# A gated mix of a diagonal state-space layer and a SiLU FFN on one core: the order of TensorE's stages, the place of its transpositions, the cut of the last readout and the choice of PSUM banks are changed

## The chip, the cores and the metric

The kernel runs on one core of one Trainium2 chip. The core has five engines that run side by side, each through its own queue in order: TensorE (PE in the profile; its weight loads are shown apart as PEld), VectorE (DVE), ScalarE (ACT), GpSimd (POOL) and SyncE (SP). SP and POOL here mostly issue DMAs. TensorE writes only to PSUM, which has eight banks of 128 partitions; VectorE or ScalarE must copy a bank out before it can be written again. The metric is the device time of one execution in microseconds (us), median of several runs; lower is better.

## The reference

The input x has 2048 tokens of 448 features. Two branches read it, and a gate mixes them token by token.

```python
g = sigmoid((x * gate_w).sum(-1))                 # one number a token
# branch a: a diagonal complex recurrence of 448 states
Lam = Lambda_re + 1j*Lambda_im;  dt = exp(log_dt);  Lam_bar = exp(dt*Lam)
B_bar = ((Lam_bar - 1)/Lam)[:, None] * (B_re + 1j*B_im)
Bu = x @ B_bar.T
for t in range(2048):  h = Lam_bar*h + Bu[t];  hs.append(h)
a = 2*real(hs @ (C_re + 1j*C_im).T) + x*Dskip
# branch b: a feed-forward layer, 448 -> 1792 -> 448
b = silu(x @ w1) @ w2
out = g*a + (1 - g)*b
```

## The kernel before

**Chunks and slots.** The tokens are taken in four chunks of 512 (tc = 0 to 3), and each chunk in four blocks of 128 (tb = 0 to 15). The 448 complex states are 896 real rows, held in seven slots of 128.

**TensorE's kinds of work.** The text uses these names:

- *xT*: 32 transpositions of 64 x 64 (line 515) that turn a chunk of x so that features lie on partitions. Two evictions of 1024 columns each (523 or 525) copy them out. Chunk 0 has its own form (478).
- *F* and *B*: the products of x with w1 and with the input matrix (line 670). Their depth of 448 features is taken as seven pieces of 64 rows, and two tiles run side by side, one in the upper and one in the lower half of the array. Two tiles make a pair that holds two neighbouring banks; a pair is 14 matmuls, eight in its first half and six in its second, and the halves of neighbouring pairs alternate. A stretch of such pairs is called an X stage. F tiles leave through SiLU on ScalarE (641), B tiles as copies to U, called UG in the profile (649, or 647 for chunk 0).
- *cp*: transpositions of the readout matrix C, 16 for one slot pair (815), followed by two scalings on ScalarE (823, 826, into two buffers ct in turn) and two on VectorE (828, 831), which make CP.
- *G*: the second FFN product of one block, 14 matmuls of 448 columns over all 128 rows (775). ScalarE scales it by 1 - g (781), and a DMA from POOL adds it to a tile in SBUF (783).
- *C*: the readout of one block, seven matmuls over all 128 rows (796). VectorE multiplies by g and adds the tile (799, called ot), and SP stores it (802).

So G and C use the array as one tile of 128 rows; xT, F, B, cp and the transpositions of the input matrix (611) use it as two tiles of 64 rows.

**VectorE's chain.** For each chunk (called lanes in the code) it rotates U by a table of cosines and sines, runs one scan a slot (737) along the 512 tokens, and rotates back to H, which C reads. The scans' results pass through POOL's DMAs to the type that the next step wants; in the last chunk ScalarE copies them (747). VectorE also makes the gate's products (xg, xd) and the evictions named above; ScalarE sums the gate (843 to 847) and scales x by it (850).

**What sets the order.** TensorE's order is written by hand at the end of the kernel. Every operation is first recorded with what it reads and writes, an estimated cost and a priority; `order()` then places them in time with these estimates. For PE it keeps the written order; for the other engines it takes, among those ready, the one with the best priority. It also chooses the PSUM banks (`place`, line 126 on): a bank is free when its last reader has ended by the estimate. The outcome is a fixed order for every engine, with semaphore waits; nothing is chosen on the chip.

TensorE's order from the first G on is: G0, cp0, G1, xT of chunk 2, cp1, G2, cp2, G3, cp3; the X stage of F1, one tile of F2, B2; G4, xT of chunk 3, G5 to G7, C0 to C3; the X stage of the rest of F2, B3; C4 to C7, G8 to G11; the X stage of F3; C8 to C11, G12 to G15, C12 to C15. The last readout, C15, is two products of 224 columns.

Of the kernel before, what the change touches and what calls it, by code (L numbers as in the profile page):

```python
# [15 lines left out]
D_MOD = 448  # L16
# [6 lines left out]
NOT = 5  # L23
# [30 lines left out]
class Plan:  # L54
# [49 lines left out]
    def order(self):  # L104
        ops = self.ops
        left = [len(o.deps) for o in ops]
        ready = {}
        lines = {e: [o for o in ops if o.eng == e] for e in self.INORDER}
        at = {e: 0 for e in self.INORDER}
        for o in ops:  # L110
            if not left[o.i] and o.eng not in self.INORDER:
                ready.setdefault(o.eng, []).append(o)
        free = {e: 0.72 for e in ("pe", "act", "dve", "pool", "sp")}
        pipe = {}
        banks = [0.0] * 8
        holder = [None] * 8
        done = []

        def earliest(o):
            t = 0.0  # L120
            for d in o.deps:
                p = ops[d]
                t = max(t, p.end + (self.HOP[p.eng] if p.eng != o.eng else 0.03))
            for x in o.ps_w:
                if x.bank is None:
                    b = place(x.n, t)
                    if b is None:
                        return None
                    t = max(t, max(banks[b:b + x.n]) + 0.1)
            return t  # L130

        def place(n, t):

            best = None
            for b in range(0, 8, n):
                if any(holder[b:b + n]):
                    continue
                at = max(banks[b:b + n]) + 0.1
                key = (max(at, t), n == 1 and holder[b ^ 1] is None, at)
                if best is None or key < best[0]:  # L140
                    best = (key, b)
            return None if best is None else best[1]

        while len(done) < len(ops):
            best = None
            cands = {e: l for e, l in ready.items()}
            for e in self.INORDER:
                if at[e] < len(lines[e]) and not left[lines[e][at[e]].i]:
                    cands[e] = [lines[e][at[e]]]
            for eng, lst in cands.items():  # L150
                f = free.get(eng, 0.0)
                cand = []
                for o in lst:
                    t = earliest(o)
                    if t is not None:
                        cand.append((max(t, f), o))
                if not cand:
                    continue
                t0 = min(c[0] for c in cand)
                o = min((c for c in cand if c[0] <= t0 + 1e-9), key=lambda c: (c[1].prio, c[1].i))[1]  # L160
                if best is None or (t0, o.i) < (best[0], best[1].i):
                    best = (t0, o)
            if best is None:
                raise RuntimeError("the plan is stuck")
            t, o = best
            o.start = t
            if o.sem is not None:
                free[o.eng] = t + o.cost
                q = "pool" if o.eng == "pool" else "hw"
                pipe[q] = max(pipe.get(q, 0.0), t + 0.9) + o.bytes / self.RATE[q]  # L170
                o.end = pipe[q] + 0.8
            else:
                o.end = t + o.cost
                free[o.eng] = o.end - self.LAP.get(o.eng, 0.0)
            if o.eng in self.INORDER:
                at[o.eng] += 1
            else:
                ready[o.eng].remove(o)
            for tk in o.ps_w:
                if tk.bank is None:  # L180
                    b = place(tk.n, t)
                    tk.bank = b
                    tk.left = tk.users
                    holder[b:b + tk.n] = [tk] * tk.n
                    if not tk.users:
                        holder[b:b + tk.n] = [None] * tk.n
                        banks[b:b + tk.n] = [o.end] * tk.n
            for tk in o.ps_r:
                tk.left -= 1
                for b in range(tk.bank, tk.bank + tk.n):  # L190
                    banks[b] = max(banks[b], o.end)
                    if tk.left == 0:
                        holder[b] = None
            done.append(o)
            for s in o.succ:
                left[s] -= 1
                if not left[s] and ops[s].eng not in self.INORDER:
                    ready.setdefault(ops[s].eng, []).append(ops[s])
        done.sort(key=lambda o: (o.start, o.i))
        self.span = max(o.end for o in done)  # L200
        return done
# [75 lines left out]
def bass_gated_mix__ssm_conv_s5__dense_activation_silu__prompt_kernel(nc, A_x, A_Lambda_re, A_Lambda_im, A_B_re, A_B_im, A_C_re, A_C_im,  # L277
               A_log_dt, A_Dskip, B_x, B_w1, B_w2, gate_w, out):
    with ExitStack() as ctx:
# [102 lines left out]
        def PE(fn, r, w, cost, tag=""):  # L382
            return P.add("pe", fn, r, w, cost, 0, tag=tag)
# [21 lines left out]
        load_w1("act", 0, 3, 4)  # L405
        for k, v in enumerate((A_log_dt, A_Lambda_re, A_Lambda_im)):
            load("sp", prm[k:k + 1, 0:448], v.rearrange("(o n) -> o n", o=1), f"prm{k}", 896)
        for k in (1, 2, 3):
            load_w1("sp", k, 0, 3)
            load_w1("sp", k, 3, 4)  # L410
        Bnat = H[3][:, :, 0:D_MOD]
# [2 lines left out]
        load("sp", Bnat[64:128, 3, :], A_B_im[384:448, :], "H3_3i", 64 * 896)  # L414
        load("sp", Bnat[:, 4:7, :], A_B_im[0:384, :].rearrange("(b p) d -> p b d", p=128), "H3_4 H3_5 H3_6", 384 * 896)
        btn = {s: [f"BT{s}_{h}" for h in range(2)] for s in range(7)}
        load_w1("sp", 4, 0, 3)
        load_w1("sp", 4, 3, 4)
        for dst, src, name in ((gwb, gate_w, "gwb"), (dkb, A_Dskip, "dkb")):
            load("sp", dst[:, :], src.rearrange("(o n) -> o n", o=1).partition_broadcast(128).rearrange("p o n -> p (o n)"),  # L420
                 name, 128 * 896)
# [178 lines left out]
        def b_transposes(s0, s1, who):  # L600

            tk = Ps(2)
            n = s1 - s0

            def mm(pe):
                for i in range(4):
                    for q in range(n):
                        o = (i * n + q) * 64
                        for h in range(2):
                            p = slice(64 * h, 64 * h + 64)  # L610
                            r = pe.transpose(bk(tk, h).bitcast(BF16)[:, o:o + 64], Bnat[p, s0 + q, XCOL[i]:XCOL[i] + 128], ident[p, p])  # L611
                return r
            PE(mm, [f"H3_{s}" for s in range(s0, s1)] + ["H3_3i", "ident"], [tk], n * 4 * 0.0285, "BT")
            for h in range(2):
                src = lambda h=h: bk(tk, h).bitcast(BF16)[:, 0:256 * n].rearrange("p (i s c) -> p i s c", i=4, s=n)
                dst = BT[:, :, :].rearrange("p i (s h c) -> p i s h c", h=2, c=64)[:, :, s0:s1, h, :]
                names = [f"BT{s}_{h}" for s in range(s0, s1)]
                if who[h] == "d":
                    DVE(lambda e, src=src, dst=dst: e.tensor_copy(dst, src()), [tk], names, 0.15 + n * 0.136, 2, "BTe")
                else:  # L620
                    ACT(lambda e, src=src, dst=dst: e.activation(dst, src(), AF.Copy), [tk], names, act_cost(256 * n), 2, "BTe")
# [76 lines left out]
        def F(tc, a=0, b=NFB):  # L698
            return [("F", tc, k) for k in range(a, b)]
# [87 lines left out]
        def readout(tb):  # L787
            tc, o = tb // 4, (tb % 4) * 128
            t0 = tb * 128
            cuts = [(0, D_MOD)] if tb + 1 < NTB else [(0, 224), (224, D_MOD)]  # L790
            for n, (a, b) in enumerate(cuts):
                tk = Ps()

                def mm(pe, tk=tk, a=a, b=b):
                    for s in range(NSLOT):
# [2 lines left out]
                PE(mm, [f"H{tc}_{s}" for s in range(7)] + [f"CP{s}" for s in range(NSLOT)], [tk], NSLOT * (0.0025 + (b - a) / 2400), f"C{tc}")  # L798
                DVE(lambda e, tk=tk, a=a, b=b: e.scalar_tensor_tensor(ot[tb % NOT][:, a:b], bk(tk)[:, 0:b - a], g[:, tb:tb + 1],  # L799
                                                                      Tb[:, tb, a:b], ALU.mult, ALU.add),  # L800
                    [tk, f"g_{tc}", f"Tb{tb}"], [f"ot{tb % NOT}{n}"] if len(cuts) == 2 else [f"ot{tb % NOT}0", f"ot{tb % NOT}1"], 0.2 + (b - a) / 960, 3, "out")
                P.add("sp", lambda e, a=a, b=b: e.dma_start(out2[t0:t0 + 128, a:b], ot[tb % NOT][:, a:b]),
                      [f"ot{tb % NOT}{n}"], [], 0.3, 1, outs[tb % NOT], 128 * 2 * (b - a), tag="st")

# [48 lines left out]
        def xt(tc, who):  # L853
            return [lambda: x_transposes(tc, who)]
# [8 lines left out]
            return [lambda tb=tb: readout(tb) for tb in tbs]  # L863

        turn_b = [lambda: b_transposes(0, 3, "da"), lambda: b_transposes(3, 7, "dd")]
        x_products(F(0, 0, 8) + B(0) + F(0, 8) + B(1), {-1: [parameters], (2, 0): turn_b[:1], 2: turn_b[1:], 7: xt(1, "da") + [lambda: lanes(0)]}, [3])
        gates(0)
        gates(1)
        lanes(1)
        for f in G(0) + cp(0) + G(1) + xt(2, "aa") + cp(1) + G(2) + cp(2) + G(3) + cp(3):  # L870
            f()
        x_products(F(1) + F(2, 0, 1) + B(2))
        gates(2)
        lanes(2)
        for f in G(4) + xt(3, "aa") + G(5, 6, 7) + C(0, 1, 2, 3):
            f()
        x_products(F(2, 1) + B(3))
        gates(3)
        lanes(3)
        for f in C(4, 5, 6, 7) + G(8, 9, 10, 11):  # L880
            f()
        x_products(F(3))
        for f in C(8, 9, 10, 11) + G(12, 13, 14, 15) + C(12, 13, 14, 15):
            f()

# [34 lines left out]
```

## Time and profile before

| | us |
|---|---|
| median of 3 runs | 144.31 |
| lowest and highest run | 143.67, 144.97 |
| the profiled execution, its own time | 143.31 |
| its span, first to last instruction | 141.5 |
| PE busy | 137.3 (97%) |
| DVE busy | 123.3 (87%) |
| ACT busy | 90.1 (64%) |
| POOL busy | 39.2 (28%) |

The span is what the trace covers; some 1.8 us of the execution's time lie around it. Busy time of PE counts from a matmul's start to the modelled end of its drain, so neighbouring matmuls overlap and a short wait between two of them need not show as idle. Starts are therefore the better ruler: in the timeline a row gives the start, the length, and in brackets the idle time before it and what ended it. The chain that ended last is read back from the last instruction, at each step to what released it.

### The profile page before, as it was taken

What the parts mean: (1) busy time and instruction counts of PE and PEld (TensorE: products, weight loads), DVE (VectorE), ACT (ScalarE), POOL (GpSimd) and SP (SyncE); (2) the same over time, 40 slices, a digit from 0 to 9 for tenths busy, and PEclk for the clock granted to TensorE, in tenths of its full rate; (3) what the DMA queues carried; (4) which work ended last, traced back from release to release, by engine and by line L of the source; (5) the groups of instructions that cost most, each with busy time, mean ns of one, the idle gap of its engine ahead of it and who ended that gap; (6) DMA issues with size and microseconds to landing.
All of it is one profiled execution on the core that took longest, in us unless ns stands there. A gap on an engine that the chain in (4) does not pass through costs nothing.

```text
span 141.5 us, 2984 instructions
## 1 busy us (share of the span) xinstructions
PE 137.3 (97%) x1192; PEld 67.2 (47%) x1192; DVE 123.3 (87%) x178; ACT 90.1 (64%) x155; POOL 39.2 (28%) x72
## 2 busy tenths in 40 slices
PE   7999999999999999999999999999999999899993
PEld 2535555545544444455554444445544444455552
DVE  0588999999999999999999999999999999793043
ACT  3268758999999997674961767895114699411300
POOL 7350003203346502038640004712422000013220
PEclk9999999999999999999999999999999999999999
DMA  4989999810528720119884001947423000212433
GB/s 135 272 228 270 349 358 270 203 33 11 91 46 137 118 35 0 37 21 130 134 148 127 0 5 24 152 92 161 76 39 59 0 0 0 73 61 33 65 67 97
DMA packets 18356, 14.71 MB, mean 104 GB/s; under 512 B 2723, under 2 KB 18214, under 8 KB 18342
## 3 DMA queue, kind: packets, MB, share of 16 engines
q0 software_dynamic: 6064, 5.51, 24.4%
q1 hardware_dynamic: 11718, 8.65, 20.8%
q10 hardware_dynamic: 560, 0.36, 0.8%
q8 instruction: 9, 0.15, 0.4%
q14 instruction: 5, 0.04, 0.1%
HBM read 7.17 MB, written 1.84 MB: 64 GB/s over the span
## 4 chain that ended last, share of the span: by engine, by line
PE 97%; DVE 1%; issue 0%; DVEq 0%
PE ps L670 45%; PE ps L775 31%; PE ps L796 15%; PE ps L463 2%; PE ps L515 1%; PE ps L611 1%; PE ps L815 1%; PE ps L478 1%; DVE ot L799 1%; PE ps L499 0%; PE ps L464 0%; PE ps L543 0%; DVEq L271 0%
## 5 line engine op out<-in xcount | busy, mean ns | idle before, releaser
L670 PE MATMUL ps<-xT,w1s 64*128 64x512 bf16 x392 | 47.6, 376 | 0.0
L775 PE MATMUL ps<-w2s,aT 128*128 128x448 bf16 x224 | 43.7, 353 | 0.5 <-DVE ot L799 0.5
L641 ACT ACTIVATE aT<-ps 128x1024 bf16<-128x1024 f32 (+1 forms) x30 | 28.7, 961 | 13.8 <-PE ps L670 13.7
L775 PEld LDWEIGHTS ps<-w2s,aT 128*128 128x128 bf16 x224 | 21.3, 98 | 21.1 <-issue 1.7
L670 PEld LDWEIGHTS ps<-xT,w1s 64*128 64x128 bf16 x392 | 20.1, 94 | 22.4 <-issue 1.1
L670 PE MATMUL ps<-xT,BT 64*128 64x512 bf16 x196 | 25.7, 376 | 0.0
L390 POOL DMA_DIRECT2D UG<-Gf x27 | 15.2, 570 | 32.9 <-DVE Gf L737 32.5
L783 POOL DMA_DIRECT2D xnat<-fe x16 | 14.0, 878 | 36.9 <-ACT fe L781 35.1
L781 ACT ACTIVATE fe<-ps,g 128x448 bf16<-128x448 f32 x16 | 10.2, 635 | 19.9 <-PE ps L775 15.7
L799 DVE SCALAR_TENSOR_TENSOR ot<-ps,g,xnat 128x448 bf16<-128x448 f32 (+1 forms) x17 | 10.9, 649 | 8.2 <-issue 6.6
L737 DVE TENSOR_TENSOR_SCAN Gf<-rc,gin,H 128x512 f32<-128x512 f32 x14 | 17.0, 1268 | 0.0
L796 PE MATMUL ps<-CP,H 128*128 128x448 bf16 (+1 forms) x91 | 16.6, 338 | 0.1
L670 PEld LDWEIGHTS ps<-xT,BT 64*128 64x128 bf16 x196 | 11.4, 94 | 10.4
L705 DVE TENSOR_TENSOR H<-UG,COS 128x3584 bf16<-128x3584 bf16 (+4 forms) x10 | 12.6, 1267 | 0.0
L796 PEld LDWEIGHTS ps<-CP,H 128*128 128x128 bf16 x91 | 8.7, 98 | 7.8 <-DVE ot L799 0.5
L649 ACT ACTIVATE UG<-ps 128x1024 bf16<-128x1024 f32 (+1 forms) x12 | 10.6, 915 | 1.8 <-PE ps L670 1.8
L390 POOL DMA_DIRECT2D UG<-UG x8 | 4.6, 580 | 23.3 <-DVE UG L647 11.8
L843 ACT ACTIVATE junk<-xg 128x448 bf16<-128x448 bf16 x16 | 9.2, 575 | 1.7 <-DVE xg L705 1.4
L850 ACT ACTIVATE xnat<-xnat,g 128x448 bf16<-128x448 bf16 x16 | 9.8, 662 | 0.2
L705 DVE TENSOR_TENSOR PO<-UG,SIN 128x1536 bf16<-128x1536 bf16 (+1 forms) x8 | 8.7, 1088 | 1.0 <-ACT UG L747 0.9
L705 DVE TENSOR_TENSOR PI<-UG,SIN 128x512 bf16<-128x512 bf16 (+2 forms) x13 | 9.2, 725 | 0.0
L737 DVE TENSOR_TENSOR_SCAN Gf<-rc,gin,H2C 128x512 f32<-128x512 f32 x7 | 8.7, 1274 | 0.0
(102 smaller groups left out, 124.8 us busy)
## 6 DMA issues: line engine op xcount, KB each, us to landing
UG<-Gf POOLq DMA_DIRECT2D x21, 128.0 KB, 2.6
xnat<-fe POOLq DMA_DIRECT2D x16, 112.0 KB, 2.5
out_dram<-ot SPq DMA_DIRECT2D x15, 112.0 KB, 1.7
w2s<-in_B_w_dram SPq DMA_DIRECT2D x1, 1568.0 KB, 11.4
xnat<-in_A_x_dram SPq DMA_DIRECT2D x3, 448.0 KB, 7.3
w1s<-in_B_w_dram SPq DMA_DIRECT2D x4, 192.0 KB, 3.5
w1s<-in_B_w_dram SPq DMA_DIRECT2D x1, 576.0 KB, 6.6
UG<-UG POOLq DMA_DIRECT2D x8, 64.0 KB, 2.6
```

What stands on the lines that cost most here:

```text
L390: P.add(q, lambda e: e.dma_start(dst, src), list(after), name.split(), 0.6 if q == "pool" else 0.5, prio, sem(), nbytes, tag="ld " + name)
L641: ACT(lambda e, src=src, dst=dst: e.activation(dst, src(), AF.Silu), [tk, "tbl"], [f"aT{tc % 2}_{m}" for m in names], act_cost(512 * n), 2 ...
L649: ACT(lambda e, src=src, dst=dst: e.activation(dst, src(), AF.Copy), [tk], [f"{un}{m}" for m in names], act_cost(512 * n), 5, "U")
L670: r = pe.matmul(bk(toks[k], b), weights(tile, p0, p0 + 64, i), xT[p0:p0 + 64, i, tc * CH:(tc + 1) * CH], start=(h == 0 and n == 0), stop=( ...
L705: DVE(lambda e: e.tensor_tensor(o, a, b, op), r, w, dve_cost(n, 2), prio, tag)
L737: DVE(lambda e, s=s, b=b, init=init: e.tensor_tensor_scan(Gf[:, s, :], rc[:, b:b + 1].to_broadcast([128, CH]), A[:, s, :], init, ALU.mult, ...
L775: r = pe.matmul(bk(tk)[:, 0:D_MOD], aT[tc % 2][:, fb, o:o + 128], w2s[:, fb, :], start=(fb == 0), stop=(fb == NFB - 1))
L781: ACT(lambda e: e.activation(f[:, :], bk(tk)[:, 0:D_MOD], AF.Copy, scale=g1[:, tb:tb + 1]), [tk, f"g1_{tc}"], [fn], act_cost(448, 1), 7, "fe")
L783: P.add("pool", lambda e: e.dma_start(Tb[:, tb, :], f[:, :], accum_op=ALU.add), [fn, f"Tb{tb}"], [f"Tb{tb}"], 0.94, 2, sem(), 115000, tag= ...
L796: r = pe.matmul(bk(tk)[:, 0:b - a], H[tc][:, s, o:o + 128], CP[:, s, a:b], start=(s == 0), stop=(s == NSLOT - 1))
L799: DVE(lambda e, tk=tk, a=a, b=b: e.scalar_tensor_tensor(ot[tb % NOT][:, a:b], bk(tk)[:, 0:b - a], g[:, tb:tb + 1], Tb[:, tb, a:b], ALU.mul ...
L850: ACT(lambda e, tb=tb: e.activation(Tb[:, tb, :], xnat[:, tb, :], AF.Copy, scale=g[:, tb:tb + 1]), [f"xd{tc}", f"g_{tc}"], [f"Tb{tb}"], ac ...
```

## The change

1. The X stage of F3 stands directly behind that of F2 and B3, as one stage; C4 to C7 and G8 to G11 follow it, and then C8 to C11 as before. The gate and lanes of chunk 3 are recorded inside this stage.
2. xT of chunk 2 moves from between G1 and cp1 into the X stage of F1, behind its third pair; xT of chunk 3 moves from between G4 and G5 into the X stage of F2, behind its second pair.
3. cp0 and cp1 stand together behind G0, cp2 and cp3 together behind G2.
4. C15 is three products of 192, 128 and 128 columns, each with its ot and its store.
5. Among banks that are free in time, `place` now prefers one that has been free for 1.2 us by the plan's estimate.
6. The first transposition of the input matrix (slots 0 to 2) no longer waits for the load of rows 384 to 448 of its imaginary part (H3_3i), which only slot 3 reads.

The remaining edits give names to numbers (`NH`, `K`, `len(w1cuts)`) and leave the program as it was.

```diff
-                key = (max(at, t), n == 1 and holder[b ^ 1] is None, at)
+                key = (max(at, t), max(at + 1.2, t), n == 1 and holder[b ^ 1] is None, at)
...
-            PE(mm, [f"H3_{s}" for s in range(s0, s1)] + ["H3_3i", "ident"], [tk], n * 4 * 0.0285, "BT")
+            PE(mm, [f"H3_{s}" for s in range(s0, s1)] + ["H3_3i"] * (s0 <= 3 < s1) + ["ident"], [tk], n * 4 * 0.0285, "BT")
...
-            cuts = [(0, D_MOD)] if tb + 1 < NTB else [(0, 224), (224, D_MOD)]
+            cuts = [(0, D_MOD)] if tb + 1 < NTB else [(0, 192), (192, 320), (320, D_MOD)]
...
-        for f in G(0) + cp(0) + G(1) + xt(2, "aa") + cp(1) + G(2) + cp(2) + G(3) + cp(3):
+        for f in G(0) + cp(0, 1) + G(1, 2) + cp(2, 3) + G(3):
             f()
-        x_products(F(1) + F(2, 0, 1) + B(2))
+        x_products(F(1) + F(2, 0, 1) + B(2), {2: xt(2, "aa")})
         gates(2)
         lanes(2)
-        for f in G(4) + xt(3, "aa") + G(5, 6, 7) + C(0, 1, 2, 3):
+        for f in G(4, 5, 6, 7) + C(0, 1, 2, 3):
             f()
-        x_products(F(2, 1) + B(3))
-        gates(3)
-        lanes(3)
+        x_products(F(2, 1) + B(3) + F(3), {1: xt(3, "aa"), 9: [lambda: gates(3), lambda: lanes(3)]})
         for f in C(4, 5, 6, 7) + G(8, 9, 10, 11):
             f()
-        x_products(F(3))
         for f in C(8, 9, 10, 11) + G(12, 13, 14, 15) + C(12, 13, 14, 15):
             f()
```

More of the change, by code (lines that the diff above doesn't have):

```diff
@@ L407, in bass_gated_mix__ssm_conv_s5__dense_activation_silu__prompt_kernel @@
             load("sp", prm[k:k + 1, 0:448], v.rearrange("(o n) -> o n", o=1), f"prm{k}", 896)
-        for k in (1, 2, 3):
+        for k in range(1, len(w1cuts) - 2):
             load_w1("sp", k, 0, 3)
@@ L416, in bass_gated_mix__ssm_conv_s5__dense_activation_silu__prompt_kernel @@
         btn = {s: [f"BT{s}_{h}" for h in range(2)] for s in range(7)}
-        load_w1("sp", 4, 0, 3)
-        load_w1("sp", 4, 3, 4)
+        load_w1("sp", len(w1cuts) - 2, 0, 3)
+        load_w1("sp", len(w1cuts) - 2, 3, 4)
         for dst, src, name in ((gwb, gate_w, "gwb"), (dkb, A_Dskip, "dkb")):
@@ L800, in readout @@
                                                                       Tb[:, tb, a:b], ALU.mult, ALU.add),
-                    [tk, f"g_{tc}", f"Tb{tb}"], [f"ot{tb % NOT}{n}"] if len(cuts) == 2 else [f"ot{tb % NOT}0", f"ot{tb % NOT}1"], 0.2 + (b - a) / 960, 3, "out")
+                    [tk, f"g_{tc}", f"Tb{tb}"], [f"ot{tb % NOT}{n}"] if len(cuts) > 1 else [f"ot{tb % NOT}{m}" for m in range(3)], 0.2 + (b - a) / 960, 3, "out")
                 P.add("sp", lambda e, a=a, b=b: e.dma_start(out2[t0:t0 + 128, a:b], ot[tb % NOT][:, a:b]),
@@ L865, in bass_gated_mix__ssm_conv_s5__dense_activation_silu__prompt_kernel @@
         turn_b = [lambda: b_transposes(0, 3, "da"), lambda: b_transposes(3, 7, "dd")]
-        x_products(F(0, 0, 8) + B(0) + F(0, 8) + B(1), {-1: [parameters], (2, 0): turn_b[:1], 2: turn_b[1:], 7: xt(1, "da") + [lambda: lanes(0)]}, [3])
+        NH = 8
+        K = NH // 2
+        x_products(F(0, 0, NH) + B(0) + F(0, NH) + B(1),
+                   {-1: [parameters], (K - 2, 0): turn_b[:1], K - 2: turn_b[1:], 7: xt(1, "da") + [lambda: lanes(0)]}, [K - 1])
         gates(0)
```

## The prediction

> **What bounds the kernel now.** I read the page's busy times first, then the chain that ended last, then TensorE's timeline, because the first two name one engine and only the third shows where that engine stands still. From the page:
>
> ```profile
> PE 137.3 (97%) x1192; PEld 67.2 (47%) x1192; DVE 123.3 (87%) x178; ACT 90.1 (64%) x155; POOL 39.2 (28%) x72
> ...
> PEclk9999999999999999999999999999999999999999
> ...
> PE 97%; DVE 1%; issue 0%; DVEq 0%
> ```
>
> TensorE is the chain: what does not shorten its own queue, or a wait in it, is worth nothing. The clock row is full throughout. So I look for time in that queue in which no product is made. From the timeline of PE (start, length with the last matmul's drain, line, shapes, count):
>
> ```profile
> 28.64 2.82 PE L775 MATMUL ps<-w2s,aT 128*128 128x448 bf16 x14
> 31.39 0.38 PE L815 MATMUL ps<-ident,H2C 56*128 56x56 bf16 x16
> 31.71 2.82 PE L775 MATMUL ps<-w2s,aT 128*128 128x448 bf16 x14
> 34.46 0.64 PE L515 MATMUL ps<-ident,xnat 64*128 64x64 bf16 x32
> 34.94 0.37 PE L815 MATMUL ps<-ident,H2C 56*128 56x56 bf16 x16
> ...
> 61.33 8.12 PE L775 MATMUL ps<-w2s,aT 128*128 128x448 bf16 x42
> 69.28 5.46 PE L796 MATMUL ps<-CP,H 128*128 128x448 bf16 x28
> 74.67 8.80 PE L670 MATMUL ps<-xT,w1s 64*128 64x512 bf16 x79
> ...
> 89.89 5.72 PE L796 MATMUL ps<-CP,H 128*128 128x448 bf16 x28
> 95.45 10.76 PE L775 MATMUL ps<-w2s,aT 128*128 128x448 bf16 x56
> ...
> 116.82 5.70 PE L796 MATMUL ps<-CP,H2C 128*128 128x448 bf16 x28
> 123.00 10.75 PE L775 MATMUL ps<-w2s,aT 128*128 128x448 bf16 x56 [0.48 <-DVE ot L799]
> ```
>
> Two losses are to be read from the starts. First, **row-mode switches**. Three G in a row take 69.28 - 61.33 = 7.95, so 2.65 each. From G0 to G1 it is 31.71 - 28.64 = 3.07, with one C transposition between, which the chain gives as 0.21 where no switch stands before it (35.10, behind the x transposition). 3.07 - 2.65 - 0.21 = 0.21 for going to 64-row tiles and back, 0.105 a switch. G4 to G5 agrees: 61.33 - 58.00 - 2.65 - 0.47 (32 x transpositions at 20.04 in the chain) = 0.21. Second, **bank waits** in the readouts. C0-C3 last 5.39 with the switch behind them, so 5.29. C4-C7 last 95.45 - 89.89 = 5.56, 0.27 more; C8-C11 123.00 - 116.82 = 6.18, 0.89 more. Less 0.01 a stage for its start, the waits are 0.26 and 0.88, 1.14 together. The page's 0.5 "<-DVE ot" is only the part in which the array was empty. The timeline of DVE shows why:
>
> ```profile
> 110.72 8.34 DVE L737 TENSOR_TENSOR_SCAN Gf<-rc,gin,H 128x512 f32<-128x512 f32 x7
> 118.97 1.45 DVE L799 SCALAR_TENSOR_TENSOR ot<-ps,g,xnat 128x448 bf16<-128x448 f32 x2
> 121.30 0.96 DVE L705 TENSOR_TENSOR PO<-UG,SIN 128x1536 bf16<-128x1536 bf16 x1 [0.88 <-ACT UG L747]
> 122.17 0.68 DVE L799 SCALAR_TENSOR_TENSOR ot<-ps,g,xnat 128x448 bf16<-128x448 f32 x1
> ```
>
> C8-C11 use banks 0, 1, 0, 1 and G12 bank 0 again. The ot that frees bank 0 for C10 starts only behind seven scans, and the one for G12 stands in DVE's queue behind a product that waits for ScalarE's copies.
>
> **The change, part by part.**
>
> *Switches.* Before there are 15 between the first G and the end: X-G0, G0-cp0-G1, G1-xT-G2, G2-cp2-G3, G3-cp3, X-G4, G4-xT-G5, C3-X, X-C4, G11-X, X-C8. After: X-G0, G0-cp0-G1, G2-cp2-G3, G3-X, X-G4, C3-X, X-C4, nine. 6 x 0.105 = **-0.63**. The moved transpositions cost TensorE what they did (0.47 and 0.21); at 20.04 the chain shows 32 of them inside a 64-row stage at just that.
>
> A rule bears on this price. The Trainium skill, "TensorEngine Tiling (Array Packing)", section Key Properties, says that changing the tiling mode drains TensorE. A full drain would be 353 - 189 = 164 ns a switch here, 0.98 for six, and the sum below would be -2.2. The trace disagrees in size: the transposition at 31.39 starts before G0's last matmul ends (31.46).
>
> *Bank waits.* In the changed build C4-C7 take banks 6, 7, 0, 1, C8-C11 3, 6, 7, 0, G12 bank 1: none is reused within its group. I place it on the clock of before. The third X stage now holds F3's 98 matmuls too (10.57 without a switch), so C4 starts at 89.89 - 0.42 (four switches by then) + 10.57 = 100.0, C8 at 100.0 + 5.3 + 10.6 = 115.9, G12 at 121.2, C12 at 131.8 (133.59 before). DVE: the four ot of C4-C7 (0.6 each, 2.34) leave the scans of lanes 2, so the step behind these starts at 97.97 - 2.34 = 95.6, and the one ahead of ot4 ends 7.5 later (97.97 to 105.48 before), at 103.1. C4 is done at 100.0 + 1.3 + 0.4 = 101.7, C7 at 105.7; then ot4, the end of H2 (2.0), ot5, ot6, ot7 run to 107.2. H2 is ready at 105.4 for 115.9; banks 7, 0, 1 are free by 107.2 for 118.5 and later. H3: lanes 3 scan from 110.3 instead of 110.72 (107.1 + 1.1 + 2.1), and from there to H3's end it was 17.9, so 128.2 at the latest, for C12 at 131.8. The queues that stand behind the moved work: ScalarE has the eviction of G9 behind its copies of the first two scans of lanes 3: the first ends at 111.5, then four copies and the eviction itself at 0.52 make 114.1, and its bank is wanted by G13 at 123.8. POOL's last accumulation (issued 134.77, landing 2.5 later, wanted by C15's first ot at 138.49) moves with G15. So **-1.14**, bounds 0 (other waits in their place) and -1.14.
>
> *Transpositions inside a 64-row stage.* Their cover is ScalarE, which copies out (two of 1.02, 1.84 back to back) between SiLU evictions of 0.92 to 1.02, one to each pair of tiles of 1.51. Four bank pairs stand for all. The X stage of F1 begins at 41.28 - 0.47 - 0.21 = 40.60. Pair 0 is done 2 x 0.86 + 0.65 later, with drain and semaphore at 43.3; from there ScalarE's queue holds three SiLU (0.92), g (0.3), two of L850 (0.57) and the copies (1.94): 49.4. TensorE wants that bank pair for pair 6 at 40.60 + 0.86 + 5 x 1.51 + 0.47 = 49.48, the others with 0.3 to spare. In the next X stage ScalarE has no L850, and the margin is 0.2. I take 0; bounds 0 and +1.84 each, the copies wholly exposed.
>
> *First B transposition.* It no longer waits for H3's imaginary half. SP issues that at 6.71, landing 3.8 later; TensorE stood 0.36 before it (10.28 in the chain). The second one waits for a load issued at 7.34 that lands 4.4 later, and starts at 11.84 either way. The stall moves; 0.
>
> *C two slots at a time.* Two ct buffers, CP on DVE: cp2 wants banks 0-1 at 37.3, freed when CP of slot 4 ends, 34.9. DVE's work is the same in another order: from 33.65 four CP (0.58), xg, an add, xd (2.3), a scan (1.13) and cp2's two CP end at 40.7, and X wants their banks at 41.46. 0; without that cover TensorE waits for the rest of it.
>
> *Readout in three.* 224 columns start (1.5 - 0.259)/13 = 0.0957 apart, 448 columns 0.189: 0.42 ns a column, so 0.082 for 192 and 0.056 for 128. The last matmul starts 7 x 0.082 + 13 x 0.056 - 13 x 0.0957 = 0.06 later and is 0.04 shorter, its ot (451 ns at 224 columns, 676 at 448) 0.10 shorter, its store some 0.03. **-0.1**; bounds -0.15 and +0.5 (below). SP has one issue more, 0.33 each, 0.39 apart.
>
> A second rule speaks against this part. The Trainium skill, "TensorE: Matmul & The Clock Gate", section Back-to-back issue gap, gives some 81 ns for a 128-column matmul with its weight load. By it the part would be 14 x 0.025 - 0.1 = +0.25, the sum -1.5.
>
> **Sum:** -0.63 - 1.14 - 0.1 = -1.87 against the profiled execution's 143.31 (span 141.5 and 1.8 around it): 141.44. The three runs' median is 144.31 (143.67 to 144.97), a us above the profiled one; taking the same off it gives **142.4**. One per cent, 1.44, is about what a measurement tells from no change, so the bound of faster is 142.87.
>
> **Rivals.** *A, the waits come back* (0.20): DVE is 87% busy and unbroken from 25 to 119, so a us of slip anywhere could put TensorE behind DVE again. Against it, margins of 3.6 and more above. Only the switches and the tail stay: 144.31 - 0.7 = 143.6. *B, slower* (0.07): ScalarE falls behind in the two X stages, and each time TensorE stands the full 1.84 of copies: +3.68 - 1.87 = +1.8, 146.1. It decides from 1.87 of new PE waits on ScalarE. For it, the margin of 0.1 at 49.48; against it, ScalarE stood idle up to 0.49 a pair in the stage at 75 to 90. *C, short matmuls wait for their loads* (0.08): a weight load of 128 columns lasts 98 ns, so 14 x 0.042 = +0.59: 143.0. For it, loads and 224-column matmuls run in step now; against it, the 64-row transpositions make a load pair every 29 ns. *D, the stall before B goes too* (0.05): 0.36 if the later load lands early: 142.0. Forecast 0.60.
>
> **Numbers.** The runs spread by 0.65 to either side, so of the forecast's 0.60 some 0.47 lies under 142.87; D adds 0.05, C 0.03, A 0.02: faster 0.57. B is slower, 0.07; the rest 0.36. Range 141.4 to 144.1: the forecast with the spread, C, D and nearly all of A; B is left out.
>
> **What would show it.** Right: PE's chain has G1-G2 and G4-G7 unbroken, C4-C7 and C8-C11 each 5.3 from start to start, no "<-DVE ot" before PE, PE busy near 135.5, span near 139.6. Wrong: a gap in X at the transposition with ScalarE's xT as its end; the last three readouts over 1.45; a C group over 5.4; H3 later than PE's C12.

## The result, and the profile after

The changed kernel takes 142.48 us (median of six runs, 142.07 to 142.95) beside 144.20 for the kernel before in the same rounds (143.37 to 144.97): a ratio of 0.9889, 95% interval 0.9848 to 0.9930. In later rounds it took 142.50 beside 143.85, ratio 0.9900 (0.9878 to 0.9922). The profiled execution took 142.07 with a span of 140.2 (before 143.31 and 141.5), at a mean granted clock of 0.998.

From the page of the changed kernel, the busy times and the engines of the chain that ended last:

```profile
PE 136.7 (97%) x1199; PEld 67.5 (48%) x1199; DVE 123.2 (88%) x179; ACT 89.0 (63%) x155; POOL 38.7 (28%) x72
...
PE 97%; DVE 0%; issue 0%
```

TensorE is still nearly the whole chain. Its timeline in the changed kernel (start, length, line, shapes, count; idle time in brackets where there is any):

```profile
28.81 2.82 PE L775 MATMUL ps<-w2s,aT 128*128 128x448 bf16 x14
...
32.08 5.47 PE L775 MATMUL ps<-w2s,aT 128*128 128x448 bf16 x28
...
40.76 5.57 PE L670 MATMUL ps<-xT,w1s 64*128 64x512 bf16 x50
46.17 0.63 PE L515 MATMUL ps<-ident,xnat 64*128 64x64 bf16 x32
46.63 4.91 PE L670 MATMUL ps<-xT,w1s 64*128 64x512 bf16 x43
...
57.95 10.77 PE L775 MATMUL ps<-w2s,aT 128*128 128x448 bf16 x56
...
100.21 5.47 PE L796 MATMUL ps<-CP,H 128*128 128x448 bf16 x28
105.51 10.76 PE L775 MATMUL ps<-w2s,aT 128*128 128x448 bf16 x56
116.11 5.46 PE L796 MATMUL ps<-CP,H2C 128*128 128x448 bf16 x28
121.40 10.76 PE L775 MATMUL ps<-w2s,aT 128*128 128x448 bf16 x56
132.00 5.50 PE L796 MATMUL ps<-CP,H 128*128 128x448 bf16 x42
```

From G0 on no row of the timeline has a bracket. G1-G2 and G4-G7 are unbroken, the x transposition stands in a 64-row stage with products before and behind it, and from the first C4 to the first G8 it is 105.51 - 100.21 = 5.30, from C8 to G12 5.29 (5.56 and 6.18 before).

The span divides into three parts: up to G0; from G0 to the first matmul of C12; from there to the end, the tail. Starts of single instructions in us (those in the fences are rounded):

| kernel | second B transposition | G0 | G0 to C12 | tail | span |
|---|---|---|---|---|---|
| before | 11.841 | 28.638 | 104.953 | 7.928 | 141.519 |
| after | 11.997 | 28.809 | 103.189 | 8.252 | 140.250 |

The middle gives **1.764**. The tail takes back **0.324**, and this execution started 0.171 later: 1.764 - 0.324 - 0.171 = 1.269, the difference of the spans. VectorE's waits differ too between the two profiles. Its rows ahead of C8 and C12 in the changed kernel:

```profile
100.42 1.23 DVE L705 TENSOR_TENSOR PO<-UG,SIN 128x2048 bf16<-128x2048 bf16 x1 [1.14 <-issue]
...
121.85 0.96 DVE L705 TENSOR_TENSOR PO<-UG,SIN 128x1536 bf16<-128x1536 bf16 x1 [1.53 <-ACT UG L747]
...
128.22 2.09 DVE L705 TENSOR_TENSOR H<-H,PO 128x2048 bf16<-128x2048 bf16 x2
```

H3 is complete at 130.32, 1.68 ahead of C12 (128.59 and 5.0 ahead before). It cost TensorE nothing here, but it asks for a test of how much VectorE can still take.

### The profile page after: what moved, and what is told of

Same layout as the page of the kernel before. It is cut to its first block, busy times and chain, and to the rows that moved or that the text cites. A ratio compares the mean times of both kernels' runs of the same rounds, so it can differ in the third digit from the quotient of the medians.

```text
span 140.2 us, 3002 instructions
## 1 busy us (share of the span) xinstructions
PE 136.7 (97%) x1199; PEld 67.5 (48%) x1199; DVE 123.2 (88%) x179; ACT 89.0 (63%) x155; POOL 38.7 (28%) x72
## 3 DMA queue, kind: packets, MB, share of 16 engines
HBM read 7.17 MB, written 1.84 MB: 64 GB/s over the span
## 4 chain that ended last, share of the span: by engine, by line
PE 97%; DVE 0%; issue 0%
PE ps L670 46%; PE ps L775 31%; PE ps L796 15%; PE ps L463 2%; PE ps L515 1%; PE ps L478 1%; PE ps L815 1%; PE ps L611 1%; PE ps L499 0%; DVE ot L799 0%; PE ps L464 0%; PE ps L543 0%
## 5 line engine op out<-in xcount | busy, mean ns | idle before, releaser
L670 PE MATMUL ps<-xT,w1s 64*128 64x512 bf16 x392 | 48.6, 380 | 0.0
L796 PE MATMUL ps<-CP,H 128*128 128x448 bf16 (+2 forms) x98 | 16.4, 326 | 0.0
L799 DVE SCALAR_TENSOR_TENSOR ot<-ps,g,xnat 128x448 bf16<-128x448 f32 (+2 forms) x18 | 10.8, 626 | 4.6 <-issue 3.3
```

Source lines behind the costliest of these rows:

```text
L670: r = pe.matmul(bk(toks[k], b), weights(tile, p0, p0 + 64, i), xT[p0:p0 + 64, i, tc * CH:(tc + 1) * CH], start=(h == 0 and n == 0), stop=( ...
L796: r = pe.matmul(bk(tk)[:, 0:b - a], H[tc][:, s, o:o + 128], CP[:, s, a:b], start=(s == 0), stop=(s == NSLOT - 1))
```

## Experiments

### The tail: the cut in three, and the queue of its stores

The last store's path, on a clock that starts at C12's first matmul: the last ot ends, SP issues the store, it lands, and the span ends 0.40 later.

| | last ot ends | store issued | landing after issue | tail |
|---|---|---|---|---|
| before (224, 224) | 5.966 | 5.995 | 1.533 | 7.928 |
| after (192, 128, 128) | 5.884 | 6.305 | 1.551 | 8.252 |

The matmuls and the last ot do gain 0.08, but SP issues the last store 0.42 after its ot (0.03 before). These are SP's issues in the changed kernel, the store of C14 first (start, length; rows from the timeline of its queue):

```profile
136.94 0.33 SPq L802 DMA_DIRECT2D out_dram<-ot  x1
...
137.32 0.44 SPq L802 DMA_DIRECT2D out_dram<-ot  x1
...
137.80 0.46 SPq L802 DMA_DIRECT2D out_dram<-ot  x1
...
138.30 0.43 SPq L802 DMA_DIRECT2D out_dram<-ot  x1
```

Each of the last three begins within 0.05 us of the end of the one before it. The cut was undone alone:

```diff
-            cuts = [(0, D_MOD)] if tb + 1 < NTB else [(0, 192), (192, 320), (320, D_MOD)]
+            cuts = [(0, D_MOD)] if tb + 1 < NTB else [(0, 224), (224, D_MOD)]
```

> The changed kernel with the last readout in two parts of 224 columns again. Theory (SP's queue): in the changed kernel the third store is issued 0.42 us after its ot has ended, because three issues of 0.43 to 0.46 us stand one behind the other on SP. With two parts the last store is issued within 0.05 us of its ot; from C12's first matmul to the end of the span it takes 7.9 us instead of 8.2, a gain of 0.3. Rival (a small store is slow by itself): the last store's time from issue to landing is what grew, and with two parts it falls below 1.5 us; issue follows the ot in both.

Tail 7.919, the last store issued 0.03 after its ot; middle 103.191. The time was 142.27 us (four runs, 141.91 to 142.62; ratio to before 0.9889, 0.9856 to 0.9922). The cut in three made the longer tail. Whether it did so by SP's queue or by the number of transfers is what the next experiment asks: it keeps the three parts and gives the middle store to ScalarE's queue.

```diff
-                P.add("sp", lambda e, a=a, b=b: e.dma_start(out2[t0:t0 + 128, a:b], ot[tb % NOT][:, a:b]),
+                P.add("act" if n == 1 else "sp", lambda e, a=a, b=b: e.dma_start(out2[t0:t0 + 128, a:b], ot[tb % NOT][:, a:b]),
```

> The changed kernel with three parts, the second part's store issued from ScalarE's queue, which is empty by then, the other two from SP's. Theory (SP's queue): the third store is issued within 0.05 us of its ot, the end comes 0.4 us earlier than in the changed kernel, 7.8 us from C12's first matmul. Rival (DMA of small rows): the stores still land late, and the tail stays 8.1 to 8.2.

SP's first and third issue for C15 in this kernel, and then ScalarE's one:

```profile
137.30 0.43 SPq L802 DMA_DIRECT2D out_dram<-ot  x1
...
137.89 0.34 SPq L802 DMA_DIRECT2D out_dram<-ot  x1
```

```profile
137.51 0.35 ACTq L802 DMA_DIRECT2D out_dram<-ot  x1
```

The third store, as narrow as before, is issued 0.03 after its ot and takes 0.34 instead of 0.43; the tail is 7.771, 0.48 less than in the changed kernel: 0.39 by the earlier issue, 0.09 by a landing of 1.46 instead of 1.55. The number of transfers is the same, so it was SP's queue. The Trainium skill, "DMA: Bandwidth & Descriptors", section Issuing engines are not separate DMA queues, says that starting DMAs on several engines saves only the issuing sequencer's time, usually small beside the transfer. The trace agrees: most of the 0.48 is time of the issuing queue. At a kernel's end it counts in full.

Three kernels were then set side by side in the same rounds: the changed one, the one with the store's edit, and a third that comes below.

> The changed kernel itself, to set the two kernels with the last but one store on ScalarE's queue beside it in the same rounds. Expected: 142.3 to 142.6 us, as in its first comparison (142.48).

> The changed kernel with the second of the last three stores issued by ScalarE's queue. Theory (the tail from C12 to the end of the span is 7.77 us in place of 8.25, and nothing else differs): 0.48 us below the changed kernel of the same rounds. Rival (the shorter tail of the one profiled execution is chance): within 0.2 us of it.

The changed kernel took 142.50 us (142.10 to 142.92), the one with the store's edit 141.86 (141.65 to 142.60), ratios to before 0.9900 and 0.9863 (0.9840 to 0.9885; in its first comparison 141.79, 0.9856, 0.9824 to 0.9889). The tails were 8.248 and 7.769 again.

### The middle: banks alone, and the order without them

The kernel before, with nothing but the new preference among banks:

```diff
-                key = (max(at, t), n == 1 and holder[b ^ 1] is None, at)
+                key = (max(at, t), max(at + 1.2, t), n == 1 and holder[b ^ 1] is None, at)
```

> The kernel before with nothing but the new rule for banks; every engine's order of instructions is as before. C4 to C7 then take banks 0 to 3, C8 to C11 banks 6, 7, 4, 5. Theory: the waits came from a bank used again within its group, so both go: C4 to G8 and C8 to G12 5.30 us each from first start to first start (before 5.56 and 6.18), 1.13 us less, some 0.992 of the time before. Rival (VectorE is the bound, the bank only showed it): the waits move to G8-G12 or to C12 (H3), and less than 0.5 us is gained.

G0 to C12 took 103.831, so 1.122 less than before and 0.642 more than in the changed kernel. Its readouts in TensorE's timeline:

```profile
91.52 5.47 PE L796 MATMUL ps<-CP,H 128*128 128x448 bf16 x28
96.83 10.76 PE L775 MATMUL ps<-w2s,aT 128*128 128x448 bf16 x56
...
118.20 5.47 PE L796 MATMUL ps<-CP,H2C 128*128 128x448 bf16 x28
123.51 10.76 PE L775 MATMUL ps<-w2s,aT 128*128 128x448 bf16 x56
```

5.31 from C4 to G8 and from C8 to G12: no wait is left, and one line of the planner took them away. What remains to the changed kernel, 0.642, is six switches at 0.107. The time was 142.97 us (142.63 to 143.82; ratio 0.9938, 0.9914 to 0.9962).

The other half, the changed kernel with the old preference:

> The changed kernel with the old rule for banks; every engine's order of instructions is that of the changed kernel. C6 then takes bank 6 behind C4, and ot4 stands on VectorE behind lanes 2, where it ran at 104.4 us although C4 was done at 101.9. Theory: C6 waits until ot4 ends at some 105.0, 2.2 us after it could start; span 142.4, no faster than before, although the six switches are saved. Rival (the new order alone takes the readouts out of the way of the scans): no wait, span 140.2 as in the changed kernel.

The middle took 104.265, 1.076 more than with the preference. Two waits, in TensorE's timeline:

```profile
104.14 2.82 PE L796 MATMUL ps<-CP,H 128*128 128x448 bf16 x14 [0.51 <-DVE ot L799]
...
119.09 4.15 PE L796 MATMUL ps<-CP,H2C 128*128 128x448 bf16 x21 [0.22 <-ACT fe L781]
```

By starts, C6 waits 0.67 for ot4, VectorE's work on C4, and C9 0.38 for a scaling of G on ScalarE. The expectation had 2.2 at C6. In this execution VectorE had no stop at 100 us, and ot4 started 74.00 after G0, in the changed kernel's profile 75.55; 0.67 + 1.55 gives the 2.2, as an estimate for an execution with that stop (what makes it is told below). The time was 143.62 us (nine runs, 143.09 to 144.54; a tenth took 145.82 and is not in the ratio; 0.9987, 0.9964 to 1.0011): without the line about banks most of the gain is gone, because the waits take back 1.08 and the tail 0.32 of the middle's 1.76.

### The margins: ScalarE at the x transposition, VectorE at C12

The first: ScalarE makes each of the two copies of chunk 2's xT twice, once more into a buffer that nobody reads. Extra work, nothing left out.

```diff
-                    ACT(lambda e, src=src, dst=dst: e.activation(dst, src(), AF.Copy), [tk], [f"xT{tc}_{h}"], act_cost(1024), 2.2, "xTe")
+                    more = H[3][:, 2 * h:2 * h + 2, :].rearrange("p a (x b n) -> p (a x) b n", x=2, b=4)
+                    ACT(lambda e, src=src, dst=dst, more=more: (tc == 2 and e.activation(more, src(), AF.Copy), e.activation(dst, src(), AF.Copy))[1],
...
```

> The changed kernel, where ScalarE makes each copy of the transposed x of chunk 2 (X stage of F1) twice: once more into a buffer that nobody reads, and then as before. The order of instructions is the same otherwise. In the changed kernel ScalarE's second copy of that stage ended at 49.54 us, and TensorE wanted its bank pair for pair 6 at about 49.65. Theory (the prediction's rival B is decided by this margin of 0.1 us): the two copies take 3.7 us more on ScalarE, TensorE waits some 1.7 us once at pair 6 (the second copy ends 3.6 us late, less what the four bank pairs take), and the stretch from G0 to C12 grows by about 1.7 us, from 103.19 to some 104.9. Rival (ScalarE's copies have slack that the margin doesn't show, since other banks can be taken): no wait over 0.3 us, the stretch stays at 103.2 to 103.4.

In the changed kernel ScalarE's row of the two copies ends at 47.60 + 1.94 = 49.54:

```profile
47.60 1.94 ACT L525 ACTIVATE xT<-ps 128x1024 bf16<-128x1024 bf16 x2
```

With the copies doubled, TensorE's timeline shows:

```profile
47.59 3.19 PE L671 MATMUL ps<-xT,w1s 64*128 64x512 bf16 x28
52.37 1.90 PE L671 MATMUL ps<-xT,w1s 64*128 64x512 bf16 x15 [1.60 <-ACT xT L526]
```

Counted from G0, the second copy ends 1.83 later than in the changed kernel (the expectation's 3.7 us is the length of all four copies, not what they add, so its wait of 1.7 was right by a wrong sum). TensorE waits 1.76 by starts, the middle takes 104.962 (+1.773), and the time was 144.76 us in one run, beside 144.09 before. So the stage had 0.07 to spare, and one delay of 1.83 there takes away what the middle had gained (104.953 before).

The second: four VectorE products more, two of 1.135 and two of 0.87 us, into dead buffers ahead of the last scans.

```diff
+                dead = [BT[:, :, :].rearrange("p a n -> p (a n)"), H[0][:, :, :].rearrange("p a n -> p (a n)")] * (tc == 3)
+                more = [(d[:, c:c + 512 * n].rearrange("p (s n) -> p s n", s=n), n) for d in dead for c, n in ((0, 4), (2048, 3))] + [(PI[:, 0:4, :], 4)]
+                DVE(lambda e: [e.tensor_tensor(d, U[:, 4:4 + n, :], SIN[:, 0:n, :], ALU.mult) for d, n in more][-1],
...
```

> The changed kernel with four VectorE products more (two of 1.135 us and two of 0.87 us, together 4.0 us, into buffers that nobody reads any more) ahead of the scans of the last lanes; nothing else differs. It asks how much margin the H3 parts have before C12, which the prediction put at 3.6 us. Theory (the profile after: H3 complete at 130.32, C12 begins at 132.0, margin 1.7): H3 is complete at about 134.3, TensorE waits about 2.3 us at C12, and the stretch from G0 to C12 is about 105.5 in place of 103.19. Rival (the margin of the prediction, 3.6 us, holds in this run too, since VectorE's waits on the way differ between executions): TensorE waits at most 0.4 us, the stretch is at most 103.6.

The theory fell: the middle was 103.189, the same to the nanosecond, and no wait stood at C12. VectorE's rows in this kernel:

```profile
99.90 1.22 DVE L705 TENSOR_TENSOR PO<-UG,SIN 128x2048 bf16<-128x2048 bf16 x1
...
124.03 0.96 DVE L705 TENSOR_TENSOR PO<-UG,SIN 128x1536 bf16<-128x1536 bf16 x1 [0.24 <-ACT UG L750]
...
130.41 2.08 DVE L705 TENSOR_TENSOR H<-H,PO 128x2048 bf16<-128x2048 bf16 x2
```

H3 was complete 0.55 ahead of C12. Set beside the changed kernel's profile, it came only 1.13 later from G0, but the two executions differ in more than the added work: the stop at 100 us, which lies ahead of the added products and can't have taken them up, is missing, and the wait for ScalarE's copies is 0.24 instead of 1.53. The stop is a wait for POOL's last load of lanes 2 (slot 6, from Gf to UG). Its size and its time from issue to landing, in the changed kernel and in the kernel with the store's edit (from the view of the DMAs, the window at the issue):

```profile
UG<-Gf POOLq DMA_DIRECT2D x1, 128.0 KB, 4.2
```

```profile
UG<-Gf POOLq DMA_DIRECT2D x1, 128.0 KB, 2.3
```

It took 4.24 to 4.32 us in three executions, the two of the changed kernel and the one in which the first transposition of B waits again (below), and VectorE's product starts 0.18 after the landing. In the ten others it took 2.20 to 2.50, and they have no such stop. The single packets in the traces show what came between. In the three, a packet of 16 KB on the instruction queue starts 68.39 to 68.58 after G0, while the load is under way, and lasts 1.56 to 1.84; the last eight of the load's 128 packets, a sixteenth, start only as it ends. In the other executions of the changed order that packet starts within 0.01 us of the end of the load's last one. POOL's accumulation of block 9 landed late in the same three too (3.85 to 4.25 us after its issue, 2.5 to 2.7 in the others of this order), and ScalarE's queue stands behind it, ahead of the copies for which VectorE waits at 121 us. All this is read from the traces; no run tests it.

So the added work has to be set beside executions without the late load. In five of them (the kernels of the tail's tests and the last kernel below) H3 is complete 98.62 to 98.77 after G0, 4.4 to 4.6 ahead of C12; with the added 4.0 us it is 102.64. The work was passed on nearly in full, 3.9 to 4.0 us. The margin is some 4.5 us where POOL's transfers land on time and 1.07 to 1.68 where they are late. No run has both the late load and the added work; 4.0 is more than 1.68, so TensorE might well wait there.

### The start: the first transposition of B, and what the spread of times is

The edit of the first transposition was undone alone:

```diff
-            PE(mm, [f"H3_{s}" for s in range(s0, s1)] + ["H3_3i"] * (s0 <= 3 < s1) + ["ident"], [tk], n * 4 * 0.0285, "BT")
+            PE(mm, [f"H3_{s}" for s in range(s0, s1)] + ["H3_3i", "ident"], [tk], n * 4 * 0.0285, "BT")
```

> The changed kernel with one part undone: the first transposition of B waits again for the 64-row load of B_im that it doesn't read. Theory (the prediction: the stall only moves): the wait is back ahead of the first transposition, the second one starts 0.09 us after the load of slots 4 to 6 lands as in every run so far, and from its start to G0 there are 16.80 us as in the changed kernel. So the part is worth 0. Rival (it takes something off the start): that distance is longer than 16.80 by the length of the first transposition's wait, up to 0.4 us.

Its two transpositions in TensorE's timeline:

```profile
10.60 0.53 PE L611 MATMUL ps<-ident,H 64*128 64x64 bf16 x24 [0.24 <-issue]
...
12.61 0.64 PE L611 MATMUL ps<-ident,H 64*128 64x64 bf16 x32 [0.83 <-issue]
```

The first wait is back, the second transposition starts 0.09 after its load landed (12.519), and G0 follows it by 16.799 (16.81 in the changed kernel). Worth 0, as predicted; one run took 142.63 us.

If that load's landing sets the start, an earlier issue should pay. The last kernel has the store's edit and this one:

```diff
+        load("sp", Bnat[:, 4:7, :], A_B_im[0:384, :].rearrange("(b p) d -> p b d", p=128), "H3_4 H3_5 H3_6", 384 * 896)
         load("sp", Bnat[0:64, 3, :], A_B_re[384:448, :], "H3_3", 64 * 896)
         load("sp", Bnat[64:128, 3, :], A_B_im[384:448, :], "H3_3i", 64 * 896)
-        load("sp", Bnat[:, 4:7, :], A_B_im[0:384, :].rearrange("(b p) d -> p b d", p=128), "H3_4 H3_5 H3_6", 384 * 896)
```

> The changed kernel with two edits: the second of the last three stores is issued by ScalarE's queue, and SyncE issues the load of B_im's slots 4 to 6 ahead of the two 64-row loads of B instead of behind them (at about 6.2 us instead of 7.4). In the runs so far the second transposition of B starts 0.09 us after that load's landing, at 11.8 to 13.5 us, and G0 16.80 us behind it. Theory (this landing sets the start of everything): the load lands about 1.1 us earlier, the 64-row loads land at about 11.0 to 11.3 and are now the last, the second transposition starts at 11.0 to 11.4 us, G0 at 27.8 to 28.2, and the time is 0.6 to 1 us below that of the kernel with the store's edit alone (141.79 us): about 141. Rival (the traffic of the loads behind it sets the landing, not the issue): the last of the three loads still lands at 11.8 us or later, and the time is that of the kernel with the store's edit alone within 0.3 us.

The large load landed at 11.17 and the last of the three at 11.55, but TensorE's second transposition started at 11.80:

```profile
10.38 0.51 PE L611 MATMUL ps<-ident,H 64*128 64x64 bf16 x24
...
11.80 0.64 PE L611 MATMUL ps<-ident,H 64*128 64x64 bf16 x32 [0.26 <-ACT BT L621]
```

A new wait took the old one's place, ScalarE's copy of the first transposition. The time was 141.97 us (141.39 to 142.21; ratio 0.9848, 0.9820 to 0.9876), no better than the store's edit alone. The two were set beside one another in the same rounds:

> The kernel with the store's edit and the earlier load of B_im. Theory (from the profiled execution of that kernel: the load no longer sets the second transposition's start, ScalarE's copy of the first one does, at 11.80 us; the start of other executions still varies with the first 10 us): 0.1 to 0.3 us below the kernel with the store's edit alone. Rival (the load's landing varied so much only in the executions that were profiled by chance, and the edit is worth nothing): within 0.1 us of it.

141.79 us (141.53 to 142.14; ratio 0.9854, 0.9831 to 0.9876), 0.07 below: by these runs the earlier load is worth nothing that can be told from zero. Both kernels with the store's edit are below the changed one, by 0.6 to 0.7 us in the medians (0.5 by the table that follows), and so below both kernels of this case.

The profiled executions tell what the spread of times is:

| kernel, execution | second B transposition | its time | difference |
|---|---|---|---|
| before | 11.84 | 143.31 | 131.47 |
| changed, first and second | 12.00, 12.86 | 142.07, 142.92 | 130.07, 130.06 |
| store's edit, first and second | 11.99, 12.35 | 141.55, 141.90 | 129.56, 129.56 |
| store's edit and earlier load | 11.80, 12.23 | 141.39, 141.78 | 129.59, 129.55 |

Behind that transposition the two profiled executions of one kernel agree to 0.04 us; what differs is when it starts. That the runs without a profile spread for the same reason is likely, but not shown. So the change itself is worth 131.47 - 130.07 = 1.40 us, by one execution of the kernel before and two of the changed one.

## Why the prediction was right, and where it was not

- **Time.** 142.4 was predicted, 142.48 and 142.50 were measured. The sum behind it, -1.87, was too large by 0.47 (-1.40 measured), of which the readout in three makes 0.42. The median that the prediction took its sum from, 144.31, was too high by about as much: later medians of the kernel before were 143.85 to 144.20, and 143.85 - 1.40 = 142.45 beside the measured 142.50 (144.20 - 1.40 = 142.80 beside 142.48 in the first comparison). Two errors cancel; that the hit is so close is luck.
- **Switches, -0.63.** Right: 0.642 between the bank rule alone and the whole change, 0.107 each. The price of 164 ns, a full drain worked out from rows, would have given 0.98; these runs show no such price. With the next term this is the whole of the middle's 1.764, so the transpositions of C in twos and the moved x transpositions cost nothing, as put down.
- **Bank waits, -1.14.** Right: -1.122 alone. C4, C8, G12 and C12 were placed at 100.0, 115.9, 121.2 and 131.8 and came at 100.21, 116.11, 121.40 and 132.00, with a start 0.17 later. Rival A, that the waits come back, did not happen; the order without the bank rule shows what it would have cost, 1.08 in the profiled execution.
- **x transpositions, 0, with 0.1 to spare.** Right, and the margin was as thin as stated: 49.54 against some 49.65 in the changed kernel, and doubled copies cost 1.77.
- **First B transposition, 0.** Right, with its mechanism: the wait moved to the second one.
- **Readout in three, -0.1.** This term was mis-sized: **+0.32**, inside the bounds of -0.15 and +0.5. The matmuls' and ot's part came as worked out (-0.08). The step that failed is "SP has one issue more, 0.33 each, 0.39 apart": the 0.33 was the length of an issue that stands alone, and behind one another they took 0.43 to 0.46 and started 0.48 to 0.50 apart, while the two narrow parts were ready 0.39 apart. Three issues in a row behind C14's left the last one to be issued 0.42 behind its ot.
- **Rival C, short matmuls that wait for their loads.** It did not happen: 128-column matmuls start 0.056 apart, as the line through 224 and 448 columns gave. The 81 ns that the Trainium skill gives for 128 columns ("TensorE: Matmul & The Clock Gate", section Back-to-back issue gap) are not what this trace shows.
- **H3 "128.2 at the latest".** That is 99.56 after G0. It was wrong in both profiles of the changed kernel (101.5 and 101.65) and right in the five executions without the late load (98.62 to 98.77). The prediction took VectorE's stretches at the lengths that they had before (7.5 to ot4, 17.9 from the scans on); the late landings are what it left out. TensorE waited in none of them, but the 3.6 us that stood against rival A were not there in every execution: the least margin was 1.07.
- **The signs.** The order and the 5.3 us came as said. PE's busy time was 136.7 in place of 135.5: in the middle it fell by only 1.15 (104.34 to 103.19), since 0.61 of what was gained there had been idle, and ahead of G0 it was 0.56 longer. The last three readouts took 1.52 from the first start to the last end, over the 1.45 that was to show the prediction wrong; its own working gives 1.5 + 0.06 - 0.04 = 1.52, so that bound was set too low.
- **Rival D, the stall before B goes too.** It did not happen. The load can be brought forward, but ScalarE's copy was next, and the time did not move by more than the runs can tell.

## What to carry to other kernels

When a tail is cut into more parts, write down when each part is ready and when its issuing queue is free: one queue that issues several DMAs in a row can cost more than the shorter last part saves, and a second queue takes that away. Judge a margin by more than one execution: here one late load made 4.5 us into 1.7, and an experiment that is set beside the wrong execution seems to show that a chain takes up delay. Compare two kernels from the same event, not from the start of the span, where a load's landing moves everything behind it.

## What the runs showed of the hardware

The issue of a store on SP's queue took 0.33 to 0.34 us where the queue had been free for 0.16 us or more (448, 224 and 128 columns), 0.37 where it had been free for 0.1 (224 columns), and 0.43 to 0.46 directly behind another (192 and 128 columns). The same store of 128 columns took 0.43 directly behind another and 0.34 otherwise, so it is not the width; why an issue behind another takes longer stays open. A load of 128 KB from POOL landed 4.24 to 4.32 us after its issue in the three executions in which its last eight packets started at the end of a 16 KB packet of the instruction queue, and 2.20 to 2.50 after it in the ten others. Ahead of G0, one load's landing varied by 1.6 us between executions: the load of slots 4 to 6 of B, issued at 7.34 to 7.37, landed between 11.75 and 13.38 in eleven of them, and with it moved the start of all that follows. Why it varies stays open.
